# Sliding-window attention into a hard-swish block: V behind its neighbours in one staging tile, and a fold in two PSUM tiles

## The chip, the cores and the metric

The kernel runs on one core of one Trainium2 chip. The metric is the device time of one execution in microseconds. Before the change three runs gave 300.36, 301.05 and 301.09 us; their median, 301.05 us, is the time before.

## The reference

Eight batches of eight heads, 576 positions, head size 64. Each position attends to itself and the 63 before it; the result, laid out as 4608 tokens by 512, goes through two matrix products with a hard-swish between them.

```python
scores = scale * np.matmul(q, k.transpose(0, 1, 3, 2))
mask = (rel >= 0) & (rel < window)
scores = np.where(mask, scores, -1000000000.0)
scores = scores - np.max(scores, axis=-1, keepdims=True)
attn = np.exp(scores)
attn = attn / (np.sum(attn, axis=-1, keepdims=True) + 1e-09)
attn_out = np.matmul(attn, v)
...
x = np.ascontiguousarray(attn_out.transpose(0, 2, 1, 3)).reshape(B * S, H * D)
h = x @ w_in
relu6 = np.clip(h + 3.0, 0.0, 6.0)
g = h * relu6 / 6.0
return (g @ w_out).astype(np.float32)
```

## The kernel before, in words

**The work.** The tokens are cut into nine tiles of 512 (t = 0 to 8). A tile has two products: `s1_part` (line 726) multiplies the attention output xT by w_in, 16 column blocks of four accumulated 128x512 matmuls (line 736), `s1_finish` applies the activation on ACT and DVE (lines 749 and 754), and `s2_part` (line 763) multiplies the result gT by w_out, four row blocks of sixteen matmuls (line 775). Attention goes batch by batch, in four head pairs g = 0 to 3, and while tile t is in its second product, batch t+1 is worked on.

**Attention of batches 0 and 1.** q and k of a head pair land as A[n], nine positions side by side on one partition. TensorE transposes them in 64x64 pieces into PSUM (the "fold": `fold_pair`, line 502, for batch 0; `fold_two`, line 526, for two head pairs of batch 1), and ACT or DVE copies them to F_[n] (lines 518 and 544). Then come the scores (line 580), exp on ACT (line 596), the mask on DVE (line 605), the product with V (`pv_rows`, line 625), the division (lines 635 and 636), a transpose (line 651) and the copy to xT (line 368). The last 64 positions of all heads are an extra item "e" (`pv`, line 677). V is kept twice: as blocks of 128 positions and as blocks shifted by 64; `shift_v` (line 456) makes the shifted half with two copies per head pair, on POOL, ACT or DVE.

**Loads.** SP loads q and ACT loads k of batch 0's first pair as f32 into stage tile 0 (`load_pair`, line 407), and DVE casts them. SP then loads V of the first two head pairs in four pieces of 128 positions into stage tile 1 (`load_tok`, line 418); `cast_v` (line 463) casts them, with copies recorded at line 368. POOL's queue casts on the way and loads all else: the other pairs of q and k (`load_cast`), V of the last two pairs (`load_vhead`, four loads), w_in in five pieces, w_out in four, then q, k and V of batch 1, then q and k of batch 2 (nq, nk). A POOL load holds one of eight semaphores, so a load is issued only when the one eight places before it has landed.

**PSUM.** Two tiles of one bank (pn), and three of two banks (pb, and two pa). `wide` gives both banks of a tile, `bank` the first alone. Before, a fold of two head pairs takes one wide tile, one bank for each pair.

**What sets the order.** The class `Plan` (line 50) gives every operation a cost and places it on its engine by earliest start; the order that comes out is fixed. The first loads have no modelled landing but fixed due times, the table `LANDED` (line 23). Where the planner may choose (`alts`), the engine of a copy and the PSUM tile come out of it too. A change of a due time can therefore move instructions far away, on all engines.

Of the kernel before, what the change touches and what calls it, by code (L numbers as in the profile page):

```python
# [11 lines left out]
BF16 = mybir.dt.bfloat16  # L12
# [8 lines left out]

WINDOW = 64
LANDED = {
    "SP": (3000, 6210, 8070, 8430, 9600),
    "POOL": (4600, 6820, 7920, 9640, 10900, 11600, 11950, 12350, 12800, 13200),
    "ACT": (3200,),
}
NEXT = (15140, 16470, 19010, 21590, 24580, 26640, 29180, 30650, 32050, 32490, 35020, 37600, 39010, 40440, 41280, 42170, 43000, 43830, 44270, 45500, 46500, 47500, 48500, 49500, 50500, 51500, 52500, 53300, 54000)
MARGIN = 300
# [20 lines left out]
class Plan:  # L50
# [13 lines left out]
    def add(self, eng, dur, emit, reads=(), writes=(), prio=0, stream=None, after=(), alts=None, port=False):  # L64
        op = Op(eng, dur, emit, reads, writes, prio, stream or eng)
        op.alts = alts
        op.port = port
        for r in reads:
            if r in self.last_w:
                op.deps.add(self.last_w[r])  # L70
            self.readers.setdefault(r, []).append(op)
        for w in writes:
            if w in self.last_w:
                op.deps.add(self.last_w[w])
            op.deps.update(self.readers.get(w, ()))
            self.last_w[w], self.readers[w] = op, []
        op.follows = {a for a in after if a is not None}
        op.deps.discard(op)
        op.seq = len(self.ops)
        self.ops.append(op)  # L80
        return op
# [141 lines left out]
def kernel(  # L223
# [9 lines left out]
    nc = tc.nc  # L233
    P = nc.NUM_PARTITIONS
    B, H, S, D = q.shape
# [5 lines left out]
    SP = KB * P  # L241
    R = S // D
# [22 lines left out]
    def wide(op, name):  # L265
        s, k = op.got[name]
        return banks[k][s]

    def bank(op, name):
        s, k = op.got[name]  # L270
        return banks[k][s][:] if k == "n" else banks[k][s][:, 0, :]

    def sb(shape, dt, name):
        return consts.tile(shape, dt, name=name)
# [5 lines left out]
    A = {n: sb([P, NG, R, D], BF16, f"A{n}") for n in "qk"}  # L280
# [6 lines left out]
    def t_key(n, b, g):  # L287
        return ("T" if b >= ROWS_FROM else "F") + n, g

    def home(b, g, h):  # L290
        return 1 - h if 0 < b < ROWS_FROM and g % 2 else h
# [48 lines left out]
    fold = sb([P, D], BF16, "fold")  # L340
# [7 lines left out]
    add = pl.add  # L348
# [4 lines left out]
    def act(n):  # L353
        return 160 + n / 1.2

    def dve(n, fast=1):
        return 150 + n / 0.96 / fast
# [4 lines left out]
    def cpy(eng):  # L362
        return {"DVE": nc.vector.tensor_copy, "ACT": nc.scalar.copy, "POOL": nc.gpsimd.tensor_copy}[eng]
# [9 lines left out]
    def pe(dur, em, reads, writes, stream, alloc=None, kinds=("n",), after=(), mode="f"):  # L373
        op = add("PE", dur, em, reads=reads, writes=writes, stream=stream, after=after)
        op.alloc, op.kinds, op.mode = alloc, kinds, mode
        return op
# [4 lines left out]
    def new_stage():  # L381
        i = nst[0] % NST
        nst[0] += 1
        return i
# [22 lines left out]
    def load_pair(n, src, b, g, i, x, eng="SP"):  # L407
        st = stage[i][:, x * R * D : (x + 1) * R * D]
        dma(P, 106, st, src[b, 2 * g : 2 * g + 2].rearrange("h (p j) d -> (h p) (j d)", j=R), writes=[("stp", n, g)], eng=eng)
        copy_op(R * D, A[n][:, g, :, :].rearrange("p j d -> p (j d)"), st, ("ACT", "DVE"),  # L410
                [("stp", n, g)], [("A", n, g)] + st_keys(i, 0, NG, range(KB)), sbuf=True, prio=700)
# [113 lines left out]

    def fold_two(n, g0, b, gate, kinds=("b", "a")):

        name = ("F", n, b, g0)
        key = ("ps", name)
        pair = (g0, g0 + 1)  # L530
        op = pe(R * 38 + 30, None, [("A", n, g) for g in pair] + ["fold"], [key], "pick", alloc=(name,), kinds=kinds, after=gate, mode="r")

        def em():
            for j in range(R):
                for g in pair:
                    for h in range(2):
                        r, o = (slice(x * D, (x + 1) * D) for x in (h, home(b, g, h)))
                        nc.tensor.transpose(out=wide(op, name).bitcast(BF16)[o, g - g0, j * D : (j + 1) * D],
                                            in_=A[n][r, g, j, :], identity=fold[r, :])

        op.emit = em

        def ev(eng, g):
            cpy(eng)(out=F_[n][:, g, :].rearrange("d (p j) -> d p j", j=R),
                     in_=wide(op, name).bitcast(BF16)[:, g - g0, 0:S].rearrange("d (j p) -> d p j", p=D))

        for g in pair:
            alts = {e: (c, (lambda e=e, g=g: ev(e, g)), False) for e, c in (("DVE", dve(S)), ("ACT", act(S) - 30))}
            e = add("DVE", 0, None, reads=[key], writes=[t_key(n, b, g)], alts=alts, stream="copy", prio=300)
            e.frees = (name,)  # L550
        return op

    def scores(b, items, gate, stream="att", pr=300, masked=False, kinds=("a",)):
# [297 lines left out]
    def hold(n, after):  # L851
# [6 lines left out]
        writes=["half", "m32"])  # L858
    add("DVE", 250, lambda: (nc.vector.memset(V[:, :, :, D : D + 2], 1.0), nc.vector.memset(V[:, :, :, 3 * D : 3 * D + 2], 1.0)),
        writes=["V1"])  # L860
    i0, iv = new_stage(), new_stage()
    load_pair("q", q, 0, 0, i0, 0)
    load_pair("k", k, 0, 0, i0, 1, "ACT")
    load_tok(v, 0, iv, 0, 2, range(NE))
# [14 lines left out]
    for e, times in LANDED.items():  # L879
# [3 lines left out]
        reads=["c32"], writes=["fold"], prio=3000)  # L883
# [25 lines left out]
    for n in "qk":  # L909
        then(add("POOL", pool(NG * P), lambda n=n: nc.gpsimd.memset(by_block(n, N_)[D:P, KB - 1, :, :], 0.0),  # L910
             writes=[("n" + n, NE, 0), ("n" + n, NE, 1)], after=chain))
# [3 lines left out]
    for t in range(NTT):  # L915
# [27 lines left out]
        b = t + 1  # L943
        if b < B:
            if b == 1:
                gate = (hs[4],)
                cast_v(iv, 0, 2, (THREE,) * 3, parts=REST, prio=-2500, pieces=(1,))
                scores(0, ("e",), gate, "pick", kinds=("b", "a"))
                pv(0, "e", None, (), "pick")
                then(load_vrows(1, NE, chain))  # L950
                for g in range(0, NG, 2):
                    for n in "qk":
                        fold_two(n, g, 1, gate)
                for g in range(NG):
                    shift_v(g, g + 1, THREE)
                attend(1, gate, gate, "pick", ROWS)
            else:
                for g in range(0, NG, 2):
                    shift_v(g, g + 2, ("ACT", "DVE") if b == 2 else ("DVE",))
                attend(b, (hs[LATE if b > ROWS_FROM else -1],), (hs[-1],))  # L960
            if b + 1 < B:
                load_rows(b + 1)
# [53 lines left out]
```

## Time and profile before

| | |
|---|---|
| median of three runs | 301.05 us (300.36 to 301.09) |
| the profiled execution | 301.96 us |
| its span, first to last instruction | 300.3 us |
| TensorE busy | 291.6 us, 97% of the span |
| ACT, DVE, POOL busy | 207.7, 197.9, 121.8 us |
| TensorE clock granted | 1.00 throughout |

The profile page gives busy time by engine, the span in 40 slices, the chain of work that ended last, and groups of equal instructions. In a line of the timeline the columns are start and duration in us, engine, line of the kernel, operation, tiles written and read, how many, and in brackets how long the engine was idle before and what ended that. A busy TensorE in this page may also be one that waits within its pipeline, so starts of matmuls tell more than its share.

### The profile page before, as it was taken

To read this page: it belongs to the slowest core of one execution; us is meant where nothing else is said; L and a number is where in the kernel's file an instruction comes from. 1 tells how busy PE (TensorE), PEld (TensorE's weight loads), DVE (VectorE), ACT (ScalarE), POOL (GpSimd) and SP (SyncE) were. 2 spreads that over 40 slices of the span, in tenths; PEclk is the share of its full clock that TensorE was granted. 3 is DMA by queue.
4 is the path that set the end of the run, shared out by engine and by line. 5 is a ranking of instruction groups with operands and counts; after the bars stand their busy time and mean duration, and the time that the engine had idled before them with its cause. 6 is when DMAs were issued, how large, how long until landed. Compare 5 with 4: busy or idle time off the path is not lost.

```text
span 300.3 us, 6970 instructions
## 1 busy us (share of the span) xinstructions
PE 291.6 (97%) x2825; PEld 153.7 (51%) x2825; DVE 197.9 (66%) x326; ACT 207.7 (69%) x324; POOL 121.8 (41%) x170
## 2 busy tenths in 40 slices
PE   7799999999999999999999999999999999999996
PEld 6554445445544554445687554455445544444443
DVE  4568637777578884878678776878587867206700
ACT  3778566878877795778687867876687857227611
POOL 8783859049628909920893059504000000000000
PEclk9999999999999999999999999999999999999999
DMA  8999999979999999979998699959901010110011
GB/s 184 189 204 203 202 191 150 187 103 128 160 181 156 129 167 185 171 52 181 151 167 56 120 172 178 88 100 172 126 0 37 37 70 1 37 70 35 0 72 70
DMA packets 137680, 36.66 MB, mean 122 GB/s; under 512 B 126256, under 2 KB 132912, under 8 KB 137648
## 3 DMA queue, kind: packets, MB, share of 16 engines
q0 software_dynamic: 98816, 17.80, 73.4%
q1 hardware_dynamic: 38688, 18.12, 25.2%
q8 instruction: 22, 0.36, 0.5%
q10 hardware_dynamic: 144, 0.29, 0.4%
q14 instruction: 10, 0.08, 0.1%
HBM read 36.70 MB, written 9.44 MB: 154 GB/s over the span
## 4 chain that ended last, share of the span: by engine, by line
PE 87%; DMA 8%; POOL 2%; issue 1%; DVE 1%; ACT 0%; DVEq 0%; POOLq 0%
PE pn L775 37%; PE pn L736 17%; PE pa L736 13%; PE pb L736 10%; DMA Ak<-in_k_dram 7%; PE pa L677 3%; PE pa L580 2%; DMA V<-in_v_dram 2%; PE pa L775 1%; POOL nq L389 1%; PE pb L677 1%; POOL nk L389 1%; PE pb L580 0%; DVE opg L636 0%; PE pa L625 0%
## 5 line engine op out<-in xcount | busy, mean ns | idle before, releaser
L775 PE MATMUL pn<-wout,gT 128*128 128x512 bf16 x560 | 129.5, 379 | 0.0
L736 PEld LDWEIGHTS <-win 128*128 128x128 bf16 x640 | 62.0, 98 | 60.5
L775 PEld LDWEIGHTS <-gT 128*128 128x128 bf16 x592 | 54.3, 98 | 57.8 <-issue 0.2
L736 PE MATMUL pn<-xT,win 128*128 128x512 bf16 (+1 forms) x276 | 62.3, 357 | 0.0
L749 ACT ACTIVATE t<-pn,half 128x512 bf16<-128x512 f32 x62 | 42.7, 689 | 9.0 <-PE pn L736 8.8
L736 PE MATMUL pa<-xT,win 128*128 128x512 bf16 (+1 forms) x208 | 48.6, 359 | 0.0
L754 DVE SCALAR_TENSOR_TENSOR gT<-t,pn 128x512 bf16<-128x512 bf16 x62 | 42.5, 686 | 8.7 <-ACT t L749 8.6
L754 DVE SCALAR_TENSOR_TENSOR gT<-t,pa 128x512 bf16<-128x512 bf16 x47 | 32.2, 687 | 24.4 <-ACT t L749 24.1
L389 POOL DMA_DIRECT2D nk<-in_k_dram x55 | 41.6, 780 | 2.9 <-DMA Tk<-nk 0.8
L389 POOL DMA_DIRECT2D V<-in_v_dram x40 | 33.2, 851 | 15.1 <-PE pa L677 12.4
L749 ACT ACTIVATE t<-pa,half 128x512 bf16<-128x512 f32 x47 | 32.1, 686 | 8.8 <-PE pa L736 8.3
L697 DVE TENSOR_TENSOR xT<-pa,rec 64x512 bf16<-64x512 f32 (+1 forms) x48 | 32.0, 667 | 9.4 <-ACT rec L686 8.4
L736 PE MATMUL pb<-xT,win 128*128 128x512 bf16 (+1 forms) x156 | 37.0, 358 | 0.0
L754 DVE SCALAR_TENSOR_TENSOR gT<-t,pb 128x512 bf16<-128x512 bf16 x35 | 24.0, 686 | 16.3 <-ACT t L749 16.3
L788 ACT COPY osb<-pn 128x512 f32<-128x512 f32 x17 | 9.9, 584 | 31.8 <-PE pn L775 31.8
L683 ACT ACTIVATE rec<-pa 64x512 f32<-64x512 f32 (+1 forms) x48 | 27.5, 573 | 5.6 <-PE pa L677 4.5
L749 ACT ACTIVATE t<-pb,half 128x512 bf16<-128x512 f32 x35 | 24.1, 690 | 7.7 <-PE pb L736 7.7
L389 POOL DMA_DIRECT2D nq<-in_q_dram x30 | 26.7, 890 | 3.3 <-DMA wout<-in_moe_w_out_dram 1.6
L596 ACT ACTIVATE pT<-pa 128x1024 bf16<-128x1024 f32 x25 | 24.6, 1021 | 2.6 <-PE pa L580 2.4
L605 DVE TENSOR_TENSOR pT<-pT,mask 128x1024 bf16<-128x1024 bf16 x28 | 18.8, 689 | 5.1 <-ACT pT L596 5.1
L677 PEld LDWEIGHTS <-V 128*128 128x128 bf16 x448 | 16.9, 98 | 7.1 <-issue 0.5
L853 POOL COPY scrap<-Tq 128x1 bf16<-128x1 bf16 x5 | 0.9, 187 | 47.4 <-DMA Tq<-nq 47.4
(98 smaller groups left out, 205.8 us busy)
## 6 DMA issues: line engine op xcount, KB each, us to landing
out_dram<-osb SPq DMA_DIRECT2D x35, 256.0 KB, 3.1
V<-in_v_dram POOLq DMA_DIRECT2D x28, 128.0 KB, 6.0
nq<-in_q_dram POOLq DMA_DIRECT2D x24, 128.0 KB, 5.3
nk<-in_k_dram POOLq DMA_DIRECT2D x41, 64.0 KB, 4.5
wout<-in_moe_w_out_dram POOLq DMA_DIRECT2D x4, 512.0 KB, 14.7
win<-in_moe_w_in_dram POOLq DMA_DIRECT2D x3, 512.0 KB, 10.8
V<-in_v_dram POOLq DMA_DIRECT2D x12, 64.0 KB, 6.2
Aq<-in_q_dram POOLq DMA_DIRECT2D x2, 288.0 KB, 14.1
```

The lines of the kernel that those rows point to most:

```text
L389: em = lambda: e.dma_start(out=out_ap, in_=in_ap)
L580: nc.tensor.matmul(to[o, home(b, g, h) if x == "e" else h, y * D : (y + 1) * D], lhsT=w, rhs=q_cols(b, r, g, j), start=not masked, stop=no ...
L596: nc.scalar.activation(out=p_[:].rearrange("p j h c -> p h j c"), in_=wide(add_far if masked else op, name)[:, :, 0 : n * D].rearrange("p ...
L605: nc.vector.tensor_tensor(out=pp, in0=pp, in1=mask[:, m0 : m0 + n, :, :].rearrange("p j h c -> p (j h c)"), op=MULT)
L677: nc.tensor.matmul(wide(op, name)[:, h, y * D : (y + 1) * D], lhsT=V[:, blk, g, h * D : h * D + P], rhs=p_[:, y, home(b, g, h) if end else ...
L683: add("ACT", act(n), lambda h=h: nc.scalar.activation(out=rc[rows[h], 0:n], in_=wide(op, name)[rows[1 - h], h, 0:n], func=LN), reads=[key] ...
L697: nc.vector.tensor_tensor(out=o, in0=a, in1=z, op=MULT)
L736: nc.tensor.matmul(bank(op, name)[:, to : to + n], lhsT=win16[:, g, fc * P : (fc + 1) * P], rhs=xT[:, g, o : o + n], start=(g == 0), stop= ...
L749: nc.scalar.activation(out=t1[ti][:], in_=bank(op, name), func=RELU, bias=half[:], scale=1.0 / 6.0)
L754: nc.vector.scalar_tensor_tensor(out=gT[:, fc, :], in0=t1[ti][:], scalar=1.0, in1=bank(op, name), op0=MIN, op1=MULT)
L775: nc.tensor.matmul(bank(op, name)[:, 0:n], lhsT=gT[:, fc, col : col + P], rhs=wout16[:, fc, js], start=(fc == 0), stop=(fc == NFC - 1))
L788: alts = {e: (f(n), (lambda e=e: cpy(e)(out=osb[oi][:, js], in_=bank(op, name)[:, 0:n])), False) for e, f in (("DVE", dve), ("ACT", act))}
```

## The change

Three edits. The stage tile of batch 0's V is now the tile of the first q and k, so that SP's four V loads, which write over the same bytes, come behind the two casts that read them. `fold_two` takes one PSUM tile for each of its two head pairs (the first bank of two tiles) where it took the two banks of one. The due times of the first loads are new.

```diff
 LANDED = {
-    "SP": (3000, 6210, 8070, 8430, 9600),
-    "POOL": (4600, 6820, 7920, 9640, 10900, 11600, 11950, 12350, 12800, 13200),
-    "ACT": (3200,),
+    "SP": (3300, 6950, 7950, 8750, 9450),
+    "POOL": (4500, 5600, 6600, 8200, 9400, 10500, 11600, 12000, 12500, 13000),
+    "ACT": (3500,),
 }
...
     def fold_two(n, g0, b, gate, kinds=("b", "a")):
-        name = ("F", n, b, g0)
-        key = ("ps", name)
         pair = (g0, g0 + 1)
-        op = pe(R * 38 + 30, None, [("A", n, g) for g in pair] + ["fold"], [key], "pick", alloc=(name,), kinds=kinds, after=gate, mode="r")
+        names = tuple(("F", n, b, g) for g in pair)
+        op = pe(R * 38 + 30, None, [("A", n, g) for g in pair] + ["fold"], [("ps", x) for x in names], "pick",
+                alloc=names, kinds=kinds, after=gate, mode="r")
         def em():
             for j in range(R):
-                for g in pair:
+                for g, x in zip(pair, names):
+                    to = bank(op, x).bitcast(BF16)
                     for h in range(2):
-                        r, o = (slice(x * D, (x + 1) * D) for x in (h, home(b, g, h)))
-                        nc.tensor.transpose(out=wide(op, name).bitcast(BF16)[o, g - g0, j * D : (j + 1) * D],
-                                            in_=A[n][r, g, j, :], identity=fold[r, :])
+                        r, o = (slice(y * D, (y + 1) * D) for y in (h, home(b, g, h)))
+                        nc.tensor.transpose(out=to[o, j * D : (j + 1) * D], in_=A[n][r, g, j, :], identity=fold[r, :])
...
-        def ev(eng, g):
+        def ev(eng, g, x):
             cpy(eng)(out=F_[n][:, g, :].rearrange("d (p j) -> d p j", j=R),
-                     in_=wide(op, name).bitcast(BF16)[:, g - g0, 0:S].rearrange("d (j p) -> d p j", p=D))
+                     in_=bank(op, x).bitcast(BF16)[:, 0:S].rearrange("d (j p) -> d p j", p=D))
...
-            e = add("DVE", 0, None, reads=[key], writes=[t_key(n, b, g)], alts=alts, stream="copy", prio=300)
-            e.frees = (name,)
+            e = add("DVE", 0, None, reads=[("ps", x)], writes=[t_key(n, b, g)], alts=alts, stream="copy", prio=300)
+            e.frees = (x,)
...
-    i0, iv = new_stage(), new_stage()
+    i0 = iv = new_stage()
     load_pair("q", q, 0, 0, i0, 0)
     load_pair("k", k, 0, 0, i0, 1, "ACT")
     load_tok(v, 0, iv, 0, 2, range(NE))
```

In the program as built, the changed order is this. SP: the first V load waits for q's landing and a DVE cast, the second for k's and a cast, the other two follow. TensorE: four more warm-up matmuls (45 for 41), and in batch 0 the second pair's q is folded ahead of the first pair's k, the second pair's k ahead of the first scores. ACT: a V cast that waits for the third and fourth V load stands ahead of the second exp. POOL: the fourth and fifth piece of w_in are issued behind two V shifts instead of ahead of and between them. In batch 1, POOL makes five of the eight V shifts (four before), ACT two (three before), DVE one; the seven loads of nq and nk still stand ahead of POOL's shifts. The two copies of a fold wait for TensorE, and two of the eight also for the copy of an earlier fold that emptied the buffer; none waits for the other copy of its own fold. From there on only buffer numbers differ.

More of the change, by code (lines that the diff above doesn't have):

```diff
@@ L526, in fold_two @@
     def fold_two(n, g0, b, gate, kinds=("b", "a")):
-        name = ("F", n, b, g0)
-        key = ("ps", name)
         pair = (g0, g0 + 1)
-        op = pe(R * 38 + 30, None, [("A", n, g) for g in pair] + ["fold"], [key], "pick", alloc=(name,), kinds=kinds, after=gate, mode="r")
+        names = tuple(("F", n, b, g) for g in pair)
+        op = pe(R * 38 + 30, None, [("A", n, g) for g in pair] + ["fold"], [("ps", x) for x in names], "pick",
+                alloc=names, kinds=kinds, after=gate, mode="r")
         def em():
             for j in range(R):
-                for g in pair:
+                for g, x in zip(pair, names):
+                    to = bank(op, x).bitcast(BF16)
                     for h in range(2):
-                        r, o = (slice(x * D, (x + 1) * D) for x in (h, home(b, g, h)))
-                        nc.tensor.transpose(out=wide(op, name).bitcast(BF16)[o, g - g0, j * D : (j + 1) * D],
-                                            in_=A[n][r, g, j, :], identity=fold[r, :])
+                        r, o = (slice(y * D, (y + 1) * D) for y in (h, home(b, g, h)))
+                        nc.tensor.transpose(out=to[o, j * D : (j + 1) * D], in_=A[n][r, g, j, :], identity=fold[r, :])
         op.emit = em
-        def ev(eng, g):
+        def ev(eng, g, x):
             cpy(eng)(out=F_[n][:, g, :].rearrange("d (p j) -> d p j", j=R),
-                     in_=wide(op, name).bitcast(BF16)[:, g - g0, 0:S].rearrange("d (j p) -> d p j", p=D))
-        for g in pair:
-            alts = {e: (c, (lambda e=e, g=g: ev(e, g)), False) for e, c in (("DVE", dve(S)), ("ACT", act(S) - 30))}
-            e = add("DVE", 0, None, reads=[key], writes=[t_key(n, b, g)], alts=alts, stream="copy", prio=300)
-            e.frees = (name,)
+                     in_=bank(op, x).bitcast(BF16)[:, 0:S].rearrange("d (j p) -> d p j", p=D))
+        for g, x in zip(pair, names):
+            alts = {e: (c, (lambda e=e, g=g, x=x: ev(e, g, x)), False) for e, c in (("DVE", dve(S)), ("ACT", act(S) - 30))}
+            e = add("DVE", 0, None, reads=[("ps", x)], writes=[t_key(n, b, g)], alts=alts, stream="copy", prio=300)
+            e.frees = (x,)
         return op
```

## The prediction

> **What bounds the kernel now.** I read the page's slices first: TensorE is 97% busy and the clock is 1.00, so nothing is won outside the places where TensorE stops. Next its waits. From 17 us to 60 us there are two, and later none of size:
>
> ```profile
> PE pa L580 <- DVE Fk L544: 0.4, 1, 0.4
> PE pa L625 <- POOL V L456: 0.3, 1, 0.3
> ```
>
> All other waits lie in the first 17 us. So the change can act on the start (to 17 us) and on batch 1's attention (31 to 54 us); what lies behind is the same work in the same order. Then the chain of waits from 17 us to 60 us (start, us, what), to see which of the two decides:
>
> ```profile
> 28.62 13.26 DMA Ak<-in_k_dram
> 41.89 0.95 issue
> 42.84 0.89 POOL nq L389
> ...
> 46.35 0.87 POOL nq L389
> 47.22 0.04 issue
> 47.27 0.89 POOL V L456
> 48.16 0.04 issue
> 48.20 0.38 PE pa L625 x10
> ```
>
> Batch 1's k lands at 41.89, POOL then issues five loads back to back, and only at 47.27 comes its V shift, for which TensorE's first pv of batch 1 waits till 48.20. No TensorE work is in this stretch: it is a chain of DMA and POOL. Last the busy table by windows (length, PE, PEld, DVE, ACT, POOL, clock, DMA share, GB/s), to see whether the DMA engines have room:
>
> ```profile
> 2.00:5.00 3.00, 2.59 (x33) 2.38 (x30) 0.59 (x2) 0.52 (x1) 2.86 (x10) 1.00 1.00 267
> 5.00:10.00 5.00, 3.60 (x122) 2.42 (x124) 2.93 (x7) 3.34 (x6) 4.52 (x7) 1.00 1.20 215
> 20.00:30.00 10.00, 10.00 (x55) 4.50 (x53) 8.18 (x14) 8.81 (x14) 3.86 (x7) 1.00 1.23 204
> ```
>
> The DMA share is 1.00 or more in every such window from 2 to 50 us. Whatever is loaded later, in one ring and in one order, lands when the bytes ahead of it are through. So 48.20 us is **DMA time**, and TensorE reaches it early.
>
> **How early.** In the timeline the "e" scores stop after six of eight matmuls at 43.65 and go on at 44.30, about 0.6 lost; the first pv stops after four of sixteen at 47.60 and goes on at 48.20, about 0.55 lost; before the last quarter of w_out, which lands at 39.04 (POOL's next issue, at 39.32, waits for it), 0.1 is lost: twelve L775 matmuls take 2.89 there, 2.76 at 34.80. Together 1.25 us: so much later TensorE could arrive, with the fold's stop gone, and the pv would still start at 48.20.
>
> **Part by part.**
>
> *The fold in two tiles.* Before, the copies of the two pairs never overlap (timeline; the bracket says who released it):
>
> ```profile
> 33.11 0.64 ACT L544 COPY Fq<-pa 128x576 bf16<-128x576 bf16 x1 [0.61 <-PE pa L538]
> 33.78 0.76 DVE L544 COPY Fq<-pa 128x576 bf16<-128x576 bf16 x1 [0.56 <-ACT Fq L544]
> ...
> 42.81 0.64 ACT L544 COPY Fk<-pa 128x576 bf16<-128x576 bf16 x1
> 43.48 0.76 DVE L544 COPY Fk<-pa 128x576 bf16<-128x576 bf16 x1 [1.29 <-ACT Fk L544]
> ...
> 44.30 0.20 PE L580 MATMUL pa<-Fq,Fk 64*128 64x64 bf16 x2 [0.39 <-DVE Fk L544]
> ```
>
> After, both start when the fold ends, 42.81, and the DVE copy ends at 43.57 in place of 44.24; TensorE's four matmuls between end at 43.65. The stop of 0.6 goes. What is late next: the pv at 47.60 comes at 47.0 and waits for POOL until 48.20. Worth: 0. The fold's 36 transposes are the same (0.48 a fold). A fold now holds two of three wide tiles, till the copies end; the next user of such a tile is a matmul group 0.97 later (four L775), longer than the 0.76 copy: 0 (at worst 0.76 - 0.97 < 0). The Trainium skill, PSUM — Partial Sum Buffer, Specifications (TRN2), says that ScalarE and VectorE may read PSUM in parallel where the banks differ; the two pairs lay in different banks before too, so by that rule it is the tile and not the bank that kept the copies apart, and if it did not hold, the stop would stay and the sum would be the same 0.
>
> *V behind the casts.* The casts of q and k end at 5.50 and 5.88 (5.04 and 5.42, 0.46 each). SP issues V from 5.9 instead of 1.27; first packets, going by k (issued 0.81, first packets in 1.5 to 2), about 1 us later, at 7.0. Nothing is queued behind on SP until the stores at 40.75. In the meantime POOL's ring has four pairs (q1, k1, q2, k2, issued 1.31 to 3.63); a pair takes 0.72 (Aq with two pairs lands 1.43 after the load before it), so it can fill 2.9 us, from its first packets at 4.25 until 7.1. The engines have work nearly throughout; the hole is where V ran while POOL's ring had not begun: between 4.0 and 4.5 the SP queue moved 350 packets, at 22 ns each (316 packets took 21.7% of 16 engines for 2 us, 7.5 to 9.5) over 16 engines 0.48 us. If POOL's ring begins sooner once V is gone, the hole closes. So the ring is late by 0 to 0.5; a gain has no source, since the share is already 1.00. I take **+0.2**, between them, because POOL's first load was issued 2.9 us ahead of its first packets, which leaves it room to start sooner. It counts in full at 48.20.
>
> *The start on TensorE.* q and k of the later pairs land up to about 2 us sooner (k1 lands at 8.43 now: issued 1.99, 6.44 to landing). But the fourth pair's V head lands at 14.19 (8.72 + 5.47), last in the same bytes, and its shift and pv are behind that. Four warm-ups more, 0.08 each, end at 4.8, ahead of the first fold at 5.56: 0. Any gain here ends at the w_out landing of 39.04 and at 48.20: 0. A loss counts beyond 1.25 (the second rival).
>
> *POOL.* Two w_in pieces are issued behind the shifts, near 14.7 in place of 12.79: the ring has w_in ahead until 19.41, so 0. In batch 1 its shifts are five: 0.88, 0.61, then three of about 0.50 (0.50 for 64x384 at 14.31). The second pv (49.55) needs the third, done at 49.3; the third pv (49.93) needs the fourth, done at 49.8: 0, at worst +0.1. The nk load behind is 0.4 later; its transposed k lands at 63.47 and is used at 67.50: 0. The first shift took 0.88 beside DVE's masks (46.49 to 47.78); free of them it would be 0.50, so -0.4 to 0; DVE's masks stand behind its V shift, which waits for the same DMA, so they stay: 0.
>
> **Sum.** 301.96 (profiled) + 0 + 0.2 + 0 + 0 = 302.16, bounds -0.4 and +0.6 (301.56 to 302.56). The profiled execution is 0.91 above the median of the runs shown; on that scale **301.25 us**, 300.65 to 301.65. The runs themselves lie 0.7 us apart, so 0.3% (0.9 us) is about what can be told from no change.
>
> **The rivals.**
>
> *Faster: the pv is not held by DMA.* If POOL's five issues move up (the 0.95 between 41.89 and 42.84 has no named releaser; its other waits for a landing take 0.28) and the V landings with them, all 1.25 us of stops go: 301.25 - 1.25 = 300.0. For: 0.95 is unexplained. Against: V's fourth piece lands only shortly before 46.06, where DVE's shift starts, and the DVE masks follow it. Chance 0.12.
>
> *Slower: V is starved.* In the DMA view the queues (packets, MB, share) share quite differently by stretch; first 4.5 to 7.5 us, then 7.5 to 9.5:
>
> ```profile
> q0 software_dynamic: 321, 0.33, 67.6%
> q1 hardware_dynamic: 1400, 0.35, 53.6%
> ...
> q0 software_dynamic: 331, 0.34, 100.2%
> q1 hardware_dynamic: 316, 0.08, 21.7%
> ```
>
> At 4.4 to 1, V's 2048 packets starting at 7.0 are through near 11.3 (before, the last lands at 11.57); at one for one beside the last pair packets and the V heads, they run as long as these, near 13 to 14. ACT's queue then stands: V cast 0.62, exp 1.02, k copy 0.65, two exps 2.04, 4.3 us behind V's last landing. The last exp ended at 16.44; with the slack of 1.25 it may end at 17.7, so the point is a landing of 13.4. At 13.9 it costs 0.5, with the ring hole of 0.5 and the shift's 0.1 302.15. Chance 0.16. The Trainium skill, DMA: Bandwidth & Descriptors, Queues, rings and completion order, says that each engine goes round its queues packet by packet; 7.5 to 9.5 agrees (316 to 331), 4.5 to 7.5 does not. By that rule V is late and this rival's 302.15 is the time.
>
> *It does not do what it says:* the copies still follow each other, and the stop at 43.65 stays. By the working above, that leaves the time: 301.25, within the forecast's band. Chance 0.02.
>
> **How the numbers follow.** Forecast 0.70; with the third, within 0.3%: 0.72. Faster by over 0.3%: 0.12, the first rival; slower by over 0.3%: 0.16, the second. The range takes in both prices and the spread of the runs: 300.0 to 302.4.
>
> **What would show it.** Right: DVE's Fk copy starts beside ACT's near 42.8; the first pv still goes on near 48.2 to 48.7, released by POOL's shift; k of batch 1 lands at 41.9 to 42.4. Wrong: that landing more than 0.5 earlier; V's last stage landing after 13.4 and the first s1 matmul later than 18.5; a new TensorE stop after 54 us.

## The result, and the profile after

The changed kernel takes **304.95 us** (median of four runs, 304.60 to 305.08) against 301.02 us of the kernel before: a ratio of **1.0133, 95% interval 1.0112 to 1.0154**, slower. Run again on another chip it took 304.14 us against 300.71 (ratio 1.0106, 1.0087 to 1.0125), so the loss is 3.9 and 3.4 us. The profiled execution took 305.08 us, its span is 303.4 us (before 301.96 and 300.3). The forecast was 301.25 us, range 300.0 to 302.4: the measured time lies 2.6 us above the range.

TensorE's waits from 8 us to 60 us come first. Of the two that the prediction showed neither is left; the longest is a new one, in the start (us in total, times, longest):

```profile
PE pa L580 <- DVE Fk L518: 3.8, 1, 3.8
```

The timeline of all engines from 4 us to 24 us shows who stood in front of that copy (the first row is the fold that the copy reads):

```profile
9.63 0.47 PE L513 MATMUL pn<-fold,Ak 64*64 64x64 bf16 x18
...
10.76 0.47 PE L513 MATMUL pa<-fold,Aq 64*64 64x64 bf16 x18
...
12.13 0.29 DVE L368 CAST V<-stage 64x256 bf16<-64x256 f32 x1 [5.68 <-DMA stage<-in_v_dram]
13.13 1.18 DVE L368 CAST V<-stage 128x512 bf16<-128x512 f32 x3 [0.71 <-DMA stage<-in_v_dram]
14.23 0.75 DVE L518 COPY Fk<-pn 128x576 bf16<-128x576 bf16 x1
15.03 0.61 PE L580 MATMUL pa<-Fq,Fk 64*128 64x64 bf16 x16 [3.80 <-DVE Fk L518]
15.09 0.62 ACT L368 CAST V<-stage 128x512 bf16<-128x512 f32 x1 [5.05 <-DMA stage<-in_v_dram]
15.62 1.02 ACT L596 ACTIVATE pT<-pb 128x1024 bf16<-128x1024 f32 x1
...
21.67 0.59 PE L736 MATMUL pn<-xT,win 128*128 128x512 bf16 x2
```

Before, the same second exp, copy of the third pair's k, third scores and first s1 matmul stood so (timeline of before, 0 to 25 us):

```profile
10.47 1.03 ACT L596 ACTIVATE pT<-pb 128x1024 bf16<-128x1024 f32 x1
...
11.38 0.65 ACT L518 COPY Fk<-pn 128x576 bf16<-128x576 bf16 x1
...
12.76 0.41 PE L580 MATMUL pa<-Fq,Fk 64*128 64x64 bf16 x16
...
17.25 0.59 PE L736 MATMUL pa<-xT,win 128*128 128x512 bf16 x2
```

In the changed kernel DVE stands idle for 5.68 us at its first V cast and for 0.71 more at the second, with the copy of the third pair's k behind them: the fold that this copy reads ran at 9.63, before TensorE stopped (TensorE's last matmul ahead of the stop begins at 11.04). ACT stands idle for 5.05 us at its V cast, with the second exp behind it (15.62; before 10.47). The first s1 matmul starts at 21.67 in place of 17.25. The chain of waits names the load that set this:

```profile
7.04 7.95 DMA stage<-in_v_dram
...
15.09 0.62 ACT V L368
15.71 0.93 ACT pT L596
```

The V pieces land at 12.10, 13.10, 13.61 and 14.99 us (before 5.31, 8.64, 9.71, 11.57), although SP issues them from 5.48 to 7.04. In the DMA view (packets, MB, share of 16 engines) this is 7.5 to 10 us, then 10 to 12.5; q1 is V, q0 is POOL's ring:

```profile
q0 software_dynamic: 283, 0.24, 74.8%
q1 hardware_dynamic: 625, 0.16, 31.9%
...
q0 software_dynamic: 984, 0.15, 82.2%
q1 hardware_dynamic: 1122, 0.28, 66.4%
```

Before, V had 1400 of its 2048 packets through between 4.5 and 7.5 us; now it moves 625 and 1122 of them in the two stretches of 2.5 us after that, beside the V heads. The windows (length, PE, PEld, DVE, ACT, POOL, clock, DMA share, GB/s) show a second thing, a granted clock below 1:

```profile
10.00:15.00 5.00, 0.95 (x27) 0.47 (x20) 2.09 (x5) 0.04 (x1) 1.53 (x3) 0.80 1.63 181
15.00:20.00 5.00, 4.19 (x95) 3.18 (x97) 3.16 (x8) 4.04 (x6) 4.40 (x8) 0.51 1.28 191
```

TensorE works 0.95 us of five, and two microseconds into its stop, at 13.03, the clock falls to 0.5; it is back at 1.00 at 19.86, 6.83 us later.

In batch 1 the edit of the fold does what it says: in the timeline of 46 to 52 us both copies start beside each other, and the "e" scores run through, 24 in one piece.

```profile
47.07 0.64 ACT L544 COPY Fk<-pa 128x576 bf16<-128x576 bf16 x1 [0.67 <-PE pb L539]
...
47.18 0.76 DVE L544 COPY Fk<-pb 128x576 bf16<-128x576 bf16 x1 [0.69 <-PE pb L539]
...
47.92 0.52 PE L580 MATMUL pa<-Fq,Fk 64*128 64x64 bf16 x24
```

### The profile page after: what moved, and what is told of

Same layout as the page of the kernel before. It is cut to its first block, busy times and chain, and to the rows that moved or that the text cites. A ratio compares the mean times of both kernels' runs of the same rounds, so it can differ in the third digit from the quotient of the medians.

```text
span 303.4 us, 6940 instructions
## 1 busy us (share of the span) xinstructions
PE 289.2 (95%) x2783; PEld 154.8 (51%) x2829; DVE 198.4 (65%) x326; ACT 207.8 (68%) x323; POOL 122.7 (40%) x171
## 3 DMA queue, kind: packets, MB, share of 16 engines
q1 hardware_dynamic: 38688, 18.12, 24.8%
## 4 chain that ended last, share of the span: by engine, by line
PE 91%; DMA 4%; issue 2%; DVE 1%; ACT 1%; SPq 0%; ACTq 0%
PE pn L775 40%; PE pn L736 18%; PE pa L736 13%; PE pb L736 10%; PE pa L677 4%; DMA stage<-in_v_dram 3%; PE pa L580 2%; DMA stage<-in_q_dram 1%; PE pa L775 1%; PE pb L677 1%; PE pb L580 1%; PE pa L625 1%; DVE opg L636 0%; PE pa L651 0%; SPq L389 0%
## 5 line engine op out<-in xcount | busy, mean ns | idle before, releaser
L775 PE MATMUL pn<-wout,gT 128*128 128x512 bf16 x532 | 125.3, 379 | 2.2 <-issue 1.1
L736 PE MATMUL pn<-xT,win 128*128 128x512 bf16 (+1 forms) x278 | 64.2, 358 | 0.4
L754 DVE SCALAR_TENSOR_TENSOR gT<-t,pn 128x512 bf16<-128x512 bf16 x64 | 43.8, 686 | 11.2 <-ACT t L749 11.1
L749 ACT ACTIVATE t<-pn,half 128x512 bf16<-128x512 f32 x64 | 44.0, 689 | 10.3 <-PE pn L736 9.7
L736 PE MATMUL pa<-xT,win 128*128 128x512 bf16 (+1 forms) x198 | 46.6, 358 | 0.3
L754 DVE SCALAR_TENSOR_TENSOR gT<-t,pa 128x512 bf16<-128x512 bf16 x46 | 31.3, 687 | 21.7 <-ACT t L749 21.5
L697 DVE TENSOR_TENSOR xT<-pa,rec 64x512 bf16<-64x512 f32 (+1 forms) x50 | 32.8, 657 | 10.0 <-ACT rec L686 9.0
L736 PE MATMUL pb<-xT,win 128*128 128x512 bf16 (+1 forms) x149 | 35.1, 356 | 0.5 <-issue 0.5
L683 ACT ACTIVATE rec<-pa 64x512 f32<-64x512 f32 (+1 forms) x50 | 28.3, 566 | 4.9 <-PE pa L677 3.7
L596 ACT ACTIVATE pT<-pa 128x1024 bf16<-128x1024 f32 x24 | 23.6, 1021 | 1.4 <-PE pa L580 1.4
```

The source lines that it names most:

```text
L596: nc.scalar.activation(out=p_[:].rearrange("p j h c -> p h j c"), in_=wide(add_far if masked else op, name)[:, :, 0 : n * D].rearrange("p ...
L683: add("ACT", act(n), lambda h=h: nc.scalar.activation(out=rc[rows[h], 0:n], in_=wide(op, name)[rows[1 - h], h, 0:n], func=LN), reads=[key] ...
L697: nc.vector.tensor_tensor(out=o, in0=a, in1=z, op=MULT)
L736: nc.tensor.matmul(bank(op, name)[:, to : to + n], lhsT=win16[:, g, fc * P : (fc + 1) * P], rhs=xT[:, g, o : o + n], start=(g == 0), stop= ...
L749: nc.scalar.activation(out=t1[ti][:], in_=bank(op, name), func=RELU, bias=half[:], scale=1.0 / 6.0)
L754: nc.vector.scalar_tensor_tensor(out=gT[:, fc, :], in0=t1[ti][:], scalar=1.0, in1=bank(op, name), op0=MIN, op1=MULT)
```

## The experiments

The theory is called A: V lands late, and what TensorE waits for stands behind V's casts in the fixed order of DVE and ACT. Its first rival is called B: the new order of folds, exps and shifts, which the new due times brought, costs the time. The runs from e6 to e10 ask which part of A costs what: the order of the queues, the fall of the clock, or the lateness itself. On the chips of the experiments the kernel before took 300.98 us (e1 to e4), 300.60 (e5 to e8) and 300.71 (e9 to e11).

### One part alone, and all but one

**e1**, the kernel before with the new `fold_two` alone:

> The fold in two tiles alone: own stage tile for V, old due times. Theory A (the loss is V landing late behind the casts, with copies that TensorE needs queued behind V's casts on DVE): no loss here, 300.4 to 301.3 us; the two copies of a fold overlap, the stop of 0.6 at 43.65 goes, and the first pv of batch 1 still starts near 48.2, since POOL's shift holds it. Rival B (the loss comes from the order that the new due times make): also no loss, the same time. If the fold by itself wins or costs, this shows it: a win of the whole stop would be 300.4, a loss would be above 301.9.

300.66 us, ratio 0.9988 (0.9973 to 1.0003): no loss, and no gain that is clear of the noise. One part of the expectation missed: the first product with V did not wait for POOL at 48.2 but started at 46.70, since batch 1's k landed at 40.05. Its profile also shows where a gain can be lost again. Here are two rows of batch 2's scores in e1, then the same two in e12, a second execution of the kernel before (timelines around 69 us):

```profile
68.73 0.64 PE L580 MATMUL pa<-Tq,Tk 64*64 64x64 bf16 x54
70.06 0.28 PE L580 MATMUL pa<-Tq,Tk 64*64 64x64 bf16 x10 [0.69 <-issue]
...
69.14 0.64 PE L580 MATMUL pa<-Tq,Tk 64*64 64x64 bf16 x54
70.05 0.28 PE L580 MATMUL pa<-Tq,Tk 64*64 64x64 bf16 x10 [0.27 <-issue]
```

TensorE arrives 0.41 us earlier in e1 and goes on at the same time: in these two executions a stop without a named releaser took the fold's gain back. The kernel before has this stop in its first profile too (0.50 us, ending at 71.31).

**e2**, the kernel before with the shared stage tile alone:

```diff
-    i0, iv = new_stage(), new_stage()
+    i0 = iv = new_stage()
```

> V in the first staging tile alone: old fold, old due times, so DVE, ACT and TensorE keep the order of before. Theory A: V lands between 12 and 15 us as in the changed kernel, the first V cast on DVE stands ahead of the second pair's k copy, TensorE stops some 3 us from about 8 us on, its clock falls to half in or behind that stop, and the time is 304 to 307 us. Rival B: the order of before is a good one and V's lateness is covered, 300.5 to 301.5 us.

305.47 us, ratio 1.0144 (1.0108 to 1.0180): this one line brings the whole loss (4.5 us on its chip). V lands at 11.76, 12.08, 12.58 and 13.96, and with the old due times and folds a wait of the same kind is on top of TensorE's waits (here the copy behind DVE's first V cast is the second pair's k):

```profile
PE pb L580 <- DVE Fk L518: 4.1, 1, 4.1
```

Here too the clock is at 0.5 for 6.83 us (12.16 to 18.99).

**e3**, the kernel before with the new table of due times alone:

> The new due times alone: own stage tile, old fold. The order at the start is that of the changed kernel, V is loaded from 1.3 us on as before. Theory A: V lands by 11.6, no long stop, 300.4 to 301.5 us. Rival B: the order costs, 303 to 305 us.

301.69 us, ratio 1.0022 (1.0003 to 1.0042): 0.2 above A's band, far below B's. In its profile the clock fell for 3.41 us (14.87 to 18.28) after a stop of 1.19 at 11.24.

**e4**, the changed kernel with a stage tile of its own for V:

```diff
-    i0 = iv = new_stage()
+    i0, iv = new_stage(), new_stage()
```

> The changed kernel with V back in a staging tile of its own: new fold, new due times; TensorE's and POOL's orders are those of the changed kernel. Theory A: the whole loss of 3.9 us is gone, 300.2 to 301.5 us, DVE's k copy of the third pair by 11 us, no fall of the clock. Rival B: the loss stays, 303.5 to 305 us.

300.70 us, ratio 1.0004 (0.9985 to 1.0023). V lands from 5.18 to 9.48, no stop reaches 1 us, the clock stays at 1.00 in the profile. B falls.

**e5**, the changed kernel with the old `fold_two`:

> The changed kernel with the old fold in one tile (late V and new due times stay). Theory A (the late V is the whole loss; the new fold works in batch 1 by itself): the start is as late as in the changed kernel (first s1 matmul near 21.7 us), and the stop in the e scores of batch 1 comes back at 0.4 to 0.6 us. If what batch 1 gives back in the changed kernel (about 1.1 us between start and end of the span) is the fold's doing, 305.8 to 306.2 us; if the wider fold is worth the 0.3 us that it gave alone, 305.0 to 305.6; if the prediction's step 'worth: 0' is right, 304.6 to 305.2.

305.84 us, ratio 1.0175 (1.0155 to 1.0195): at the lower edge of the first band. The stop in the "e" scores is back, 0.57 at 47.64 from start to start. Three pairs differ by the fold alone: before and e1 (0.3 us, not clear of the noise), e3 and e4 (1.0), e5 and the changed kernel (0.9 by the medians; they ran on two chips, and against before on each chip it is 1.3 to 1.8). So it is worth 0.3 to 1.0 us, more by the last pair; the stop it removes is 0.57, and why two of the pairs show more than that was not found.

### The order of the queues, the clock, the lateness

**e8**, the changed kernel with V's casts behind the copies in the finished order:

```diff
     order = pl.settle(rank, 8)
+    last = next(op for op in order if op.writes == [("Fk", 3)])
+    casts = [op for op in order[: order.index(last)] if op.eng in ("DVE", "ACT") and op.writes[0][0] == "V" and op.writes[0][1] == 0]
+    for op in casts:
+        order.remove(op)
+    at = order.index(last) + 1
+    order[at:at] = casts
```

> The changed kernel with one thing moved: the casts of batch 0's first V pieces on DVE and ACT stand behind the copies of the third pair's k and the fourth pair's q and k, and not ahead of them; every other order is as it was. V's bytes come as late as in the changed kernel. Theory A3 (the queue order): the stop of 3.80 us goes or moves to the first product with V (near 15.7), first s1 matmul at 19.3 to 20.5, 302.5 to 303.9 us. Theory A4 (V's landing decides): 304.3 to 305.3 us.

302.38 us, ratio 1.0072 (1.0045 to 1.0100): A3, 0.1 below its band, with the first s1 matmul at 18.42, sooner than it said. The stop of 3.80 is gone from TensorE's waits, and 1.1 is left at the first product with V:

```profile
PE pa L625 <- DVE V L368: 1.1, 1, 1.1
```

The timeline shows the copy done before V is there; then DVE turns to V:

```profile
9.81 0.76 DVE L518 COPY Fk<-pn 128x576 bf16<-128x576 bf16 x1 [3.83 <-ACT Fq L518]
...
11.54 1.52 DVE L368 CAST V<-stage 64x256 bf16<-64x256 f32 x4
...
14.00 0.66 PE L625 MATMUL pa<-V,pT 128*64 128x65 bf16 x8 [1.08 <-DVE V L368]
```

It stands 1.8 us over before on its chip, the changed kernel 3.9 and 3.4 on its two: so by the medians 1.6 to 2.1 us of the loss is the order alone. The runs of e8 spread widely (301.05 to 304.44), and in its profile V's last piece landed at 13.50, sooner than the 14.99 shown above. A second count takes that out: from V's last landing to the first s1 matmul it is 4.92 us here, 5.00 in e7 and 4.90 in e9, which have the copies first too, and 6.68 in the changed kernel, 6.93 in e11 and 6.85 in e5: 1.7 to 2.0 us by the order.

**e7**, the changed kernel with the due times at the measured landings, so that the planner makes that order itself:

```diff
-    "SP": (3300, 6950, 7950, 8750, 9450),
-    "POOL": (4500, 5600, 6600, 8200, 9400, 10500, 11600, 12000, 12500, 13000),
+    "SP": (3300, 11100, 12100, 12600, 14000),
+    "POOL": (4500, 6000, 6850, 7550, 9700, 10700, 12300, 13600, 14300, 14750),
```

> The changed kernel with the table of due times set to the landings that its own trace shows (V at 11.1, 12.1, 12.6 and 14.0, less a 1 us that the planner adds; the ring's loads likewise), so that the planner itself puts the copies that TensorE waits for ahead of V's casts. V's bytes come as late as in the changed kernel. Theory A3 (most of the loss is the order on DVE and ACT, which wait for V with ready copies behind them): the stop of 3.80 us before the scores of the third pair is under 1, first s1 matmul at 19.0 to 20.3, 302.3 to 303.8 us. Theory A4 (V's landing itself decides, the order only moves the stop to the first product with V): 304.3 to 305.3 us.

305.00 us, ratio 1.0162 (1.0132 to 1.0192): by the time A4, by the trace neither. The stop went as A3 said and the first s1 matmul came at 20.30, but two other things took the gain. The clock fell later, from 18.12 to 24.95, so that it lay on the s1 matmuls, two of them in 1.06 us in place of 0.59; and in batch 1 the planner now gave DVE two V shifts behind its masks (2.14 us from 49.55; one shift before the masks in the changed kernel), and the first product with V waited there:

```profile
21.16 1.06 PE L736 MATMUL pn<-xT,win 128*128 128x512 bf16 x2
...
51.17 0.38 PE L625 MATMUL pa<-V,pT 128*64 128x65 bf16 x12 [0.88 <-DVE V L456]
```

The profiled execution was the slowest of four (306.62), and two of the others ran at a mean clock of 1.00 and still took 305.00; what they lost by was not profiled. A new table of due times is not one change but many, so e7 does not speak against e8.

**e6**, the changed kernel with TensorE kept busy in its stop:

```diff
+    into = next(op for op in order if op.alloc == (("F", "k", 0, 3),))
+    gap = next(op for op in order if op.eng == "PE" and op.writes == [("ps", ("S", 0, 2))] and not op.alloc)
...
+            if op is gap:
+                for _ in range(48):
+                    warm(into)
```

> The changed kernel with 48 matmuls of 96 columns more (their result is not used) between the fold of the fourth pair's q (ends 11.2 us) and the scores of the third pair (15.03), so that TensorE works through its stop of 3.80 us. V lands as late as before. Theory A1 (the fall of the granted clock to 0.5 is a cost of its own, beside the wait): the clock stays at 1.00, the first s1 matmul comes near 20.3 to 21.0 in place of 21.67, and the time is 303.5 to 304.3 us. Theory A2 (the queues of DVE and ACT set the end of the start, and the half clock lies beside them): 304.6 to 305.3 us, whatever the clock.

303.47 us, ratio 1.0106 (1.0085 to 1.0126), the clock at 1.00 in the profile (two of the four runs had a mean of 0.994, and they are the two longer ones, 303.71 and 304.00 against 302.77 and 303.22):

```profile
10.00:15.00 5.00, 3.42 (x100) 3.17 (x101) 3.04 (x7) 1.12 (x2) 1.84 (x3) 1.00 1.72 191
15.00:20.00 5.00, 3.42 (x95) 2.45 (x95) 4.10 (x11) 4.02 (x6) 4.89 (x8) 1.00 1.22 190
```

That is the lower edge of A1's band, with the first s1 matmul at 19.99, sooner than A1 said; but V's last piece landed at 13.78 in this profile. Counted from the end of ACT's V cast to the first s1 matmul, the changed kernel takes 21.67 - 15.71 = 5.96 us and this one 19.99 - 14.50 = 5.49: so the half clock cost about 0.5 there, by one execution of each.

**e9**, e8 with 30 such matmuls ahead of the first product with V:

```diff
+            if op.alloc == (("O", 0, 0),):
+                for _ in range(30):
+                    warm(op)
```

> The kernel with the copies first (casts of V behind the copies that TensorE waits for) and 30 matmuls of 96 columns more, whose result is not used, ahead of the first product with V, where TensorE stopped for 1.08 us and the clock fell to 0.5 from 13.63 to 20.46 us. V's bytes come as late as in the changed kernel. If the half clock is a cost of its own there (dense work lies in it: products with V, turns, the first s1 matmuls), the clock stays at 1.00 and 0.6 to 1.5 us are won over the kernel with the copies first: 300.9 to 301.8 us, and the remainder against before is the lateness of V alone. If the clock costs nothing there: 302.0 to 302.8 us. If the clock falls all the same, nothing follows for its price.

302.60 us, ratio 1.0049 (1.0029 to 1.0069); the clock was at 1.00 in all five runs. By the time the clock costs nothing (e8 took 302.38 on another chip), but the profile has a new stop in the last product with V, which the profile puts down to no engine:

```profile
18.08 0.32 PE L625 MATMUL pb<-V,pT 128*64 128x65 bf16 x8 [1.19 <-issue]
```

So e9 settles nothing on the clock: what it may have won there it lost in this stop. The price of the half clock stays between nothing and about 1 us.

**e10**, the changed kernel with one V cast on POOL, ahead of its loads of the V heads; the point is the landing, not the time:

```diff
+    cast = next(op for op in order if op.writes[:1] == [("V", 0, 0, 2)])
+    order.remove(cast)
+    cast.emit = cast.alts["POOL"][1]
+    order.insert(next(i for i, op in enumerate(order) if op.writes[:1] == [("V", 2, 0, 0)]), cast)
```

> The changed kernel with one V cast moved from ACT to POOL, ahead of the four loads of V heads, so that POOL's ring has nothing beside V but the fourth pair's q and k until V has landed. Its time is not the point (the V heads come later, 305 to 308 us). Theory S (V is late because the engines serve what POOL issued beside it): V's last stage landing at 10.8 to 12.3 us, 2 us or more ahead of the 14.99 of the changed kernel. Theory O (V's queue takes that long by itself): 13.3 to 15.2 us, as in the changed kernel and its other variants.

308.24 us, ratio 1.0247 (1.0226 to 1.0267). V's last piece landed at 12.53, 0.2 outside S's band and 0.8 below O's. In the eight other profiles with the shared tile it landed between 13.50 and 15.30. What POOL issues behind the fourth pair, the V heads first and then w_in, thus costs V 1 to 2.8 us; the rest, 5.9 us from the last issue (6.65), stays with nothing beside it but the end of the third pair's and the fourth pair's q and k.

**e11**, the changed kernel again:

> The changed kernel once more, on the same chip as the two others, to have its time beside theirs and to see how far V's landings and the fall of the clock repeat. All theories: 304.4 to 305.4 us; V's last stage landing between 13.5 and 15.0 us, clock at 0.5 for 6.83 us, between 12 and 21 us.

304.14 us (303.75 to 305.40), 0.3 below the band. V landed last at 14.78, the stop was 3.96 us, and the clock was at 0.5 from 14.81 to 21.64, 1.8 us later than in the first profile.

**e12**, the kernel before again, one execution:

> The kernel before once more, for a second profile of it. The prediction took 48.20 us, where batch 1's first product with V waits for POOL's shift behind the landing of batch 1's k (41.89), for a time that the transfers set. If that is so, the landing comes within 0.5 us of 41.89 and the wait of about 0.5 us is there again; if it is a matter of one execution, the landing comes earlier by 1 us or more and the wait is gone, with the time unchanged within 0.3 per cent. The stop of about 0.6 us in the e scores of batch 1 is there in both cases, and the first s1 matmul at 17.0 to 17.6 us.

300.73 us, span 299.0. Batch 1's k landed at 40.46, 1.43 sooner than in the profile that the prediction read, and the wait for POOL was gone; the first product with V (timeline, 40 to 49.5 us) ran its sixteen matmuls in one piece:

```profile
45.84 3.10 POOL L456 COPY V<-V 64x384 bf16<-64x384 bf16 x4
...
47.11 0.45 PE L625 MATMUL pa<-V,pT 128*64 128x65 bf16 x16
```

The stop in the "e" scores was there again (43.24, 0.57 us).

## Why the prediction was wrong, point by point

**V behind the casts, +0.2: the step that failed.** The sum followed V's transfer to what it does to POOL's ring, and took it as bounded by 0.5. It did not ask where V's casts stand in the order of DVE. The price was there: a late V holds a copy for which TensorE waits 3.80 us. The ring seems mis-sized too: the last V head landed at 15.73 for 14.19, batch 1's k at 43.64 for 41.89, 1.5 to 1.8 late and not 0 to 0.5. But e2, with the stage tile alone, has 15.12 and 41.69, and the kernel before in e12 has 13.69 and 40.46, so single executions differ by as much as these figures.

**The start on TensorE, 0.** It took the fourth V head as the last arrival. In the changed kernel V's last stage piece lands nearly as late as the V heads (14.99, against 15.73), the chain of waits above runs through it, and the first s1 matmul is 4.4 us late.

**The rival "V is starved" was the mechanism, with too small a price.** It had the sharing of the queues and even its point, a landing of 13.4. (SP issued V from 5.48, where 5.9 was forecast, but no packet of V ran before 7.5, where 7.0 was.) Two sizes were off. It let the landing end near 14 (at most "13 to 14"); it came at 14.99, which by the rival's own working is 14.99 - 13.4 = 1.6 in place of 0.5, and 303.25 us for 302.15: still 1.7 below the measured 304.95. And it counted ACT's queue alone, 4.3 us behind V; that DVE held the third pair's k copy, and with it a fold, two score groups and two exps, was not in it. Undoing that order (e8) gives 1.6 to 2.1 us back. Both signs that it named came: a landing after 13.4, first s1 matmul later than 18.5. The Trainium skill's rule that was weighed there (DMA: Bandwidth & Descriptors, Queues, rings and completion order) leads to a late V, as happened; its one for one is near the trace only from 10 to 12.5 us (1122 to 984 packets), and not in the 2.5 us before that (625 to 283).

**"The clock is 1.00, so nothing is won outside the places where TensorE stops."** True of the kernel before; the prediction carried it over to a kernel with a longer stop. The clock fell in every profile with the late V but e6 and e9, which fill the stop. What it costs could not be separated well: about 0.5 us by e6's trace. The reading of the waits in the same paragraph, "later none of size", left out the 0.50 us in batch 2's scores at 71.31, the stop that in e1 took the gain back.

**The fold, worth 0.** Mechanism right: copies side by side, the stop gone, the second tile free of cost. The size was wrong, 0.3 to 1.0 us or more; it was put at 0 because of the next point.

**"48.20 is DMA time", and 1.25 us of slack.** This was read from one execution. In a second one (e12) the transfers were 1.4 us ahead and nothing waited for POOL; what TensorE had left to give there was the 0.57 of the fold's stop. The rival "the pv is not held by DMA" was right in this, but the stop that is left to win is the fold's 0.57, not 1.25. POOL, worth 0, held: its first four shifts (3.14 from 49.03) cover the products from 51.31 with no stop.

**What stays open.** With the order put right 1.8 to 1.9 us remain against before (e8, e9). V's and the V heads' later landings are the likely cause; that was argued from the stop of 1.1 at the first product with V, not tried alone, and the half clock may be part of it (in e8's profile it lasted from 13.63 to 20.46, over the first s1 matmuls). Why V's queue needs 5.9 us from its last issue even beside two loads was not found either.

## What to carry to other kernels

When an edit delays a load, list for each engine the instructions that wait for it in the fixed order, and price what stands behind them, before the bytes: here ready copies stood behind a cast that had no data. Due times in a planner's table are a promise; where a load can slip, put the consumers of what has already landed first. And read a wait that is to cover a loss from two executions, since a transfer may be 1.4 us earlier in the next.

## What the runs showed of the hardware that was not expected

- The granted clock goes to 0.5 about 2 to 4 us into a stop of about 4 us (13.03 after a last matmul begun at 11.04; 12.16 after 8.53 in e2; 14.81 after 10.89 in e11) and stays there for 6.83 us, well beyond the stop's end; in e10 it stayed 10.24 us. It also fell after much shorter stops: in e8 at 13.63, in a stop of 1.08, and in e3 for 3.41 us after a stop of 1.00 (1.19 from start to start). In the 3.41 us ahead of the fall TensorE was busy for 1.33 us in the changed kernel, 2.03 in e3 and 2.32 in e8; what share is enough to keep the clock was not measured. Matmuls of no use in the stop kept it at 1.00 in the profile of e6 and in all five runs of e9.
- Five stops of TensorE without a named releaser (0.34 to 1.19 us idle, in e3, e4, e8 and twice in e9) each end 1.2 to 1.4 us after a 16 KB transfer of the kind "instruction" (e9: transfer 15.70 to 16.66, TensorE on at 18.08). The stop in batch 2's scores, ten to fifteen matmuls ahead of their end, is of the same kind: it stands in eleven of the fourteen profiles (0.16 to 0.92 us idle) and ends 1.3 to 1.6 us after such a transfer (e1: transfer to 68.48, TensorE on at 70.06). That TensorE waited there for its own instructions is suggested by this, not shown.
